# Another order and another choice of engine for the steps of a causal attention with a squared-ReLU layer

## The chip, the cores and the metric

The kernel runs on one core of one Trainium2 chip. The metric is device time in microseconds (us) of one execution; lower is better. Before the change the median of 3 runs is 615.8 us (615.54 to 616.38).

A core has five engines with an instruction queue each: TensorE (PE; its weight loads are shown apart as PEld), VectorE (DVE), ScalarE (ACT), GpSimd (POOL) and SyncE (SP), which issues the transfers. Each works through its own queue in order and waits for the others by semaphores.

## The reference

Causal attention over 4 batches of 12 heads (448 rows, 64 columns per head), then a two-layer block with squared ReLU on the joined heads (1792 rows of 768, 2048 in the middle). All arrays are float32.

```python
scores = scale * np.matmul(q, k.transpose(0, 1, 3, 2))
scores = np.where(mask, -1000000000.0, scores)          # causal
scores = scores - np.max(scores, axis=-1, keepdims=True)
attn = np.exp(scores)
attn = attn / (np.sum(attn, axis=-1, keepdims=True) + 1e-09)
attn_out = np.matmul(attn, v)
x = attn_out.transpose(0, 2, 1, 3).reshape(B * S, H * D)
h = x @ w_in
r = np.maximum(h, 0.0)
return (r * r) @ w_out
```

## The kernel before

**Numbers in halves.** Most operands of a matrix product are float32 values kept as two float16 tiles: a high half, which is the value scaled and rounded, and a low half, which is what the rounding left. A product is three float16 matmuls (high by high, high by low, low by high). Such pairs of steps are made everywhere: of the scaled q and k (tile qs), of v (vp), of the softmax rows (psrc, from the float32 rows pq), of the hidden layer (g, from r), of the weights (wi, wo) and of sums that the last block needs. The function `hi` makes a high half, on ScalarE (line 438) or with one TENSOR_SCALAR on VectorE or GpSimd (line 440). The function `lo` makes a low half. With a fixed scale it is one TENSOR_TENSOR on VectorE or GpSimd (line 446). With a scale per row it is one SCALAR_TENSOR_TENSOR on VectorE (line 451), but two instructions on GpSimd (lines 454 and 456):

```python
            if e == "dve":
                nc.vector.scalar_tensor_tensor(
                    out=out(), in0=in_(), scalar=scale(), in1=top(), op0=ALU.mult, op1=ALU.subtract)
            else:
                nc.gpsimd.tensor_scalar(
                    out=in_(), in0=in_(), scalar1=scale(), scalar2=1.0, op0=ALU.mult, op1=ALU.mult)
                nc.gpsimd.tensor_tensor(out=out(), in0=in_(), in1=top(), op=ALU.subtract)
```

A low half reads its high half, so it comes after it, on whatever engine that was.

**Stages.** The first batch's attention (function `early`, lines 884 to 978) runs while the weights arrive and are narrowed (lines 1022 to 1028), measured and split into halves (lines 1037 to 1115). The two layers of a block of 256 or 128 rows follow (first layer line 1300, second layer line 1319), with the attention of the next batch interleaved: scores (lines 774 and 789), row minimum on VectorE (line 757) with an accumulator read of its own, exponential on ScalarE (line 761), the sum and its inverse on VectorE (lines 801 and 804), the halves of the softmax rows, a transposing transfer (line 676), and the product with v (line 823), read out on VectorE (lines 836 and 839). The last 512 rows are computed with seven products in place of eight (lines 1583, 1685 and 1779), for which VectorE makes sums of weights and rows (line 1455) from the middle of the run on. The scaling of a row of probabilities in `early` is `scaled` (lines 646 and 648), the squares of the hidden layer are lines 1264 and 1266, the copies out of PSUM lines 1257, 1259, 1604 and others.

**What sets the order.** The code first records all 3191 steps with what each reads and writes. It then emits them in the order that a table of numbers, `ORDER`, gives; a second table, `WHERE`, gives the engine of each of the steps that may run on more than one (a ScalarE, d VectorE, g GpSimd). Buffers, transfers, shapes and dependences come from the recording and not from the tables. GpSimd reads and writes SBUF alone; steps with an operand in PSUM go to VectorE or ScalarE.

Of the kernel before, what the change touches and what calls it, by code (L numbers as in the profile page):

```python
# [23 lines left out]
    181 0 2 3 1 4 6 5 11 12 10 176 8 182 183 184 26 27 28 33 31 32 7 9 36 29 34 37 30 35 13 14 15 16 17 18 19 20 186  # L24
    21 22 38 39 40 237 196 50 51 23 24 25 177 53 45 52 201 43 41 56 57 191 44 54 46 47 48 49 42 247 55 178 389 63 58
    64 75 76 388 396 179 65 187 59 82 70 78 68 66 77 81 188 67 79 69 71 238 73 60 80 88 83 72 74 239 189 61 89 62 100
    386 390 84 197 90 387 391 101 240 95 102 103 107 85 91 93 198 98 397 92 94 104 192 105 96 106 99 193 113 180 185
    232 97 202 108 190 114 125 194 109 115 126 248 120 127 132 86 118 128 116 199 119 123 121 252 87 129 195 130 242
    122 138 200 203 124 110 249 139 117 204 145 111 150 140 770 257 151 146 205 152 153 147 157 141 143 112 156 131
    206 148 144 398 399 400 401 402 250 149 207 403 133 404 142 303 158 208 134 405 233 293 159 163 209 154 234 135  # L30
    155 210 164 235 166 406 136 211 253 288 165 407 170 137 213 411 167 214 169 160 243 254 168 244 171 161 258 412
    771 215 162 245 172 413 259 298 395 216 217 304 173 414 416 415 218 294 255 417 260 174 418 175 289 392 313 219
    220 423 393 308 421 290 221 772 773 419 295 424 299 291 222 223 236 241 246 251 224 774 296 305 422 420 342 394
    256 225 226 261 425 435 262 337 436 300 263 437 227 428 438 264 429 306 439 301 228 292 297 440 775 302 307 347
    352 314 229 776 441 265 426 443 444 230 266 777 442 427 779 445 231 446 778 430 315 447 431 787 432 448 309 267
    433 269 270 310 316 343 434 452 271 453 464 362 311 408 268 454 272 348 465 344 357 449 409 455 273 466 457 467
    472 468 312 345 456 349 469 458 353 473 317 274 350 470 275 459 590 363 318 471 354 276 474 462 475 460 463 355
    358 461 319 277 476 364 721 788 278 600 279 493 359 477 494 338 360 481 501 496 280 339 482 365 495 483 281 585
    320 340 497 282 486 595 341 346 351 356 361 366 502 591 484 498 410 592 283 487 485 601 367 450 499 284 488 451
    500 285 503 368 593 489 723 286 504 611 491 212 369 321 370 322 490 371 505 287 492 478 586 602 323 522 789 506  # L40
    587 722 793 724 510 479 725 523 588 325 790 531 480 606 780 511 525 524 507 326 727 530 512 596 603 526 726 513
    327 794 729 515 621 328 597 612 516 514 527 589 528 607 517 627 598 529 508 791 329 728 532 730 731 518 520 792
    799 733 533 616 330 795 521 519 324 608 509 534 535 594 599 331 551 609 539 604 732 734 332 628 540 610 541 735
    613 372 373 333 737 653 800 544 542 545 334 543 552 614 335 736 546 739 801 802 803 336 658 536 622 549 374 547
    835 375 623 617 554 553 796 548 738 806 555 741 624 550 740 376 537 560 797 559 556 568 618 668 743 569 805 812
    576 654 377 571 378 804 784 619 742 557 745 615 655 558 663 577 620 625 379 561 811 605 798 380 562 626 629 538
    669 381 570 807 656 744 630 563 746 836 382 747 817 631 659 749 674 947 813 564 670 632 383 781 814 660 633 572
    815 634 818 384 573 635 748 661 816 637 574 751 750 565 753 695 385 575 679 808 638 566 809 567 671 664 578 824
    579 639 580 752 640 810 581 754 657 582 755 757 665 689 823 675 583 819 820 584 676 680 681 837 666 756 758 759
    821 761 684 825 826 822 641 830 829 682 827 642 760 951 1607 958 950 954 956 955 762 828 838 643 763 662 839 764  # L50
    840 765 644 667 672 881 841 636 645 1609 953 949 882 952 842 843 844 831 1608 832 766 690 782 646 859 850 857 860
    833 647 957 768 691 685 692 677 767 971 696 969 858 686 851 834 965 967 960 964 861 1006 852 678 970 963 959 1003
    1610 862 974 673 972 687 973 876 683 648 769 688 1611 693 1004 649 875 694 697 1007 698 699 966 962 700 849 1001
    1043 863 948 1002 976 1045 650 702 1005 883 874 981 983 864 651 1613 979 873 785 701 977 703 984 652 1033 1034
    1037 1038 961 1044 982 853 978 1077 980 865 1046 705 1008 985 986 989 1047 884 866 1078 1013 1612 877 891 706 987
    994 1036 1011 707 1009 992 1039 1040 1035 867 892 1015 1075 1615 1010 708 968 1076 1012 1014 1016 885 1079 995
    1050 988 993 893 868 894 1017 1107 975 1042 996 783 990 1057 1114 1115 1018 1112 709 1053 1055 896 897 854 1021
    855 1054 710 1051 1052 1058 1026 1056 1616 991 1019 856 711 1146 1113 869 1024 712 898 1020 713 1059 1082 1116
    1041 1619 1060 1147 1025 1027 714 997 1144 870 1110 886 878 1066 1109 1028 1087 1083 1022 1089 1068 998 1090 899
# [1880 lines left out]
```

## Time and profile before

| | us |
|---|---|
| Median of 3 runs | 615.8 |
| Profiled execution, whole | 619.99 |
| its span, first to last instruction | 618.3 |
| TensorE busy | 588.2 (95%) |
| VectorE busy | 565.4 (91%) |
| ScalarE busy | 392.9 (64%) |
| GpSimd busy | 137.4 (22%) |

The profile is of one execution. Its span is 1.7 us shorter than the whole of that execution, and that execution is 4.2 us above the median of the runs. Times within the span count from its first instruction. Ends of matmuls are modelled, so that TensorE can stand as busy while it waits for a short time. TensorE's granted clock is 0.86 of full speed over the first 50 us and 1.00 after that.

### The profile page before, as it was taken

The numbers are of one execution on the slowest core, as the hardware profiler recorded it, in microseconds if no ns is written. First come the engines' busy times: TensorE is split into PE (matmuls) and PEld (weight loads), VectorE is DVE, ScalarE is ACT, GpSimd is POOL, SyncE is SP. The second block draws the span as 40 slices with busy tenths as digits, with TensorE's granted clock in tenths as the row PEclk, the third lists the DMA queues.
The fourth block names the chain that finished last, engine by engine and source line by source line (L and its number), as shares of the span: only waits on it lengthen the run. The fifth ranks groups of instructions, "written<-read, shape, count | busy, mean of one in ns | idle before, by whom it ended". The sixth has DMA issues, their size and how long they took to land. (4 is left out here: it accounts for less than half of the span.)

```text
span 618.3 us, 14173 instructions
## 1 busy us (share of the span) xinstructions
PE 588.2 (95%) x5215; PEld 438.1 (71%) x5215; DVE 565.4 (91%) x1527; ACT 392.9 (64%) x1004; POOL 137.4 (22%) x169
## 2 busy tenths in 40 slices
PE   4789999999999999999989999999999999999997
PEld 2556677888755688767878667777786768886664
DVE  4799999999999898999999998888999999999995
ACT  3688888857884676867878777776535236345420
POOL 1112111312425151231523124162310011100010
PEclk9699999999999999999999999999999999999999
DMA  9879577686668897988988979785340000000003
GB/s 221 263 243 283 191 265 267 211 255 116 139 150 168 190 172 143 210 176 198 208 161 184 177 171 191 156 165 132 65 91 14 27 2 1 14 1 1 1 1 116
DMA packets 207557, 88.71 MB, mean 143 GB/s; under 512 B 192128, under 2 KB 202368, under 8 KB 207488
## 3 DMA queue, kind: packets, MB, share of 16 engines
q1 hardware_dynamic: 207344, 87.71, 59.0%
q8 instruction: 41, 0.67, 0.5%
q14 instruction: 28, 0.23, 0.1%
q10 hardware_dynamic: 144, 0.10, 0.0%
HBM read 49.94 MB, written 5.51 MB: 90 GB/s over the span
## 5 line engine op out<-in xcount | busy, mean ns | idle before, releaser
L1300 PE MATMUL bank<-xt,wi 128*128 128x256 f16 (+1 forms) x1728 | 168.0, 255 | 1.0 <-DVE xt L1222 0.7
L1300 PEld LDWEIGHTS <-wi 128*128 128x128 f16 x1728 | 145.0, 98 | 17.7 <-issue 2.0
L1319 PE MATMUL bank<-wo,g 128*128 128x384 f16 x864 | 151.2, 326 | 0.9 <-ACT xt L1372 0.6
L1319 PEld LDWEIGHTS <-g 128*128 128x128 f16 x864 | 82.2, 98 | 52.2 <-issue 2.3
L761 ACT ACTIVATE pq<-bank,nm 112x336 f32<-112x336 f32 (+3 forms) x144 | 70.1, 491 | 48.8 <-DVE nm L757 41.1
L451 DVE SCALAR_TENSOR_TENSOR psrc<-pq,nm,psrc 112x112 f16<-112x112 f32 (+3 forms) x121 | 62.9, 545 | 1.2 <-ACT psrc L438 0.5
L757 DVE CUSTOM_DVE_ANT_0 bank<-bank,mask,sc 112x112 f32<-112x112 f32 (+3 forms) x96 | 46.9, 510 | 9.2 <-PE bank L774 8.1
L438 ACT ACTIVATE psrc<-pq,nm 112x224 f16<-112x224 f32 (+3 forms) x74 | 36.9, 525 | 8.6 <-DMA pt<-psrc 2.5
L446 POOL TENSOR_TENSOR g<-r,g 128x512 f16<-128x512 f32 x17 | 27.6, 1629 | 47.6 <-ACT g L438 44.9
L774 PE MATMUL bank<-qk 128*112 128x112 f16 (+3 forms) x192 | 32.4, 284 | 2.9 <-ACT pq L761 2.8
L823 PE MATMUL bank<-pt,vp 112*64 112x224 f16 (+3 forms) x504 | 31.1, 268 | 1.1 <-DVE xt L839 0.7
L440 POOL TENSOR_SCALAR psrc<-pq,nm 112x112 f16<-112x112 f32 (+3 forms) x25 | 16.6, 667 | 69.1 <-DVE nm L804 40.4
L823 PEld LDWEIGHTS <-vp 112*64 112x64 f16 x504 | 23.7, 109 | 10.4 <-issue 6.1
L1583 PEld LDWEIGHTS <-wi 128*128 128x128 f16 x288 | 28.2, 98 | 3.9
L761 ACT ACTIVATION_READ_ACCUMULATOR pq<-bank,nm 112x1 f32 x144 | 28.7, 199 | 0.0
L774 PEld LDWEIGHTS <-qk 128*112 128x112 f16 x192 | 21.1, 130 | 10.2 <-issue 5.3
L1264 ACT ACTIVATE r<-r 128x512 f32<-128x512 f32 x37 | 22.9, 626 | 6.0 <-DVE p L466 3.0
L913 DVE CUSTOM_DVE_ANT_0 bank<-bank,mask 128x128 f32<-128x128 f32 (+3 forms) x48 | 21.7, 485 | 5.3 <-PE bank L905 4.8
L1257 ACT ACTIVATE r<-bank 128x512 f32<-128x512 f32 x34 | 20.0, 590 | 7.6 <-DVE g L446 2.5
L757 DVE CUSTOM_DVE_ANT_0 bank<-bank,mask,vst 112x224 f32<-112x224 f32 (+3 forms) x48 | 23.0, 506 | 0.9 <-PE bank L789 0.9
L454 POOL TENSOR_SCALAR pq<-pq,nm 112x224 f32<-112x224 f32 (+3 forms) x23 | 15.6, 679 | 33.9 <-ACT psrc L438 22.7
L905 PE MATMUL bank<-wo 64*96 64x256 f32 (+4 forms) x144 | 18.5, 379 | 3.6 <-ACT wo L654 3.5
(291 smaller groups left out, 1273.7 us busy)
## 6 DMA issues: line engine op xcount, KB each, us to landing
raw<-in_moe_w_out_dram SPq DMA_DIRECT2D x8, 768.0 KB, 4.8
xt<-in_moe_w_out_dram SPq DMA_DIRECT2D x8, 768.0 KB, 5.4
xt<-in_moe_w_in_dram SPq DMA_DIRECT2D x11, 512.0 KB, 5.0
raw<-in_moe_w_in_dram SPq DMA_DIRECT2D x9, 512.0 KB, 4.9
vn<-in_v_dram SPq DMA_DIRECT2D x21, 192.0 KB, 3.0
raw<-in_v_dram SPq DMA_DIRECT2D x18, 224.0 KB, 3.5
out_dram<-ob SPq DMA_DIRECT2D x18, 192.0 KB, 2.2
raw<-in_k_dram SPq DMA_DIRECT2D x12, 224.0 KB, 4.1
```

What stands on the lines that cost most here:

```text
L438: nc.scalar.activation(out=o, in_=i, func=ACTF.Copy, scale=s)
L446: return plan.add({"dve": dve_ns(n), "pool": pool2_ns(n)}, lambda e: engines[e].tensor_tensor(out=out(), in0=in_(), in1=top(), op=ALU.subt ...
L451: nc.vector.scalar_tensor_tensor(out=out(), in0=in_(), scalar=scale(), in1=top(), op0=ALU.mult, op1=ALU.subtract)
L757: one("dve", dve_ns(w, 1, 2) - 52, lambda e: nc.vector.tensor_tensor_reduce(out=s.ap[0:P, 0:w], in0=s.ap[0:P, 0:w], in1=mask[0:P, MZ + P - ...
L761: one("act", act_ns(w, True, 1, True), lambda e: nc.scalar.activation(out=p32[j].ap[0:P, b0 * P:b0 * P + w], in_=s.ap[0:P, 0:w], func=ACTF ...
L774: nc.tensor.matmul(out=s.ap[0:P, 0:(c + 1) * P], lhsT=qT.ap[:, j * NCH + c, :], rhs=kT.ap[:, a:a + c + 1, :].rearrange("p a t -> p (a t)") ...
L823: nc.tensor.matmul(out=pv.ap[j * D:(j + 1) * D, ca * P:t1], lhsT=vp.ap[:, hv, vb:vb + D], rhs=pT[j].ap[0:P, hp * ns + x:hp * ns + x + w, : ...
L913: one("dve", dve_ns(w, 1, 1) - 52, lambda e, c=c, j=j, w=w, ss=ss, nm=nm: nc.vector.tensor_tensor_reduce(out=ss[j].ap[0:M, 0:w], in0=ss[j] ...
L1264: nc.scalar.activation(out=r.ap[:, 0:n], in_=r.ap[:, 0:n], func=ACTF.Square)
L1300: nc.tensor.matmul(out=h.ap[:, y * n:(y + 1) * n], lhsT=wi_hl(ci, hw)[:, mc], rhs=x[:, kd, hx, off:off + n], start=(kd == 0 and hw == 0 an ...
L1319: nc.tensor.matmul(out=o.ap[:, 0:HALF], lhsT=gsl(kf, hg, tt * 128, (tt + 1) * 128), rhs=wo_hl(kf, hw)[:, hh * HALF:(hh + 1) * HALF], start ...
L1583: nc.tensor.matmul(out=ps.ap[:, y * n:(y + 1) * n], lhsT=A[0](f, kd, hw)[:, mc], rhs=B[0](kd, hx), start=(first and y == 0 and kd == 0 and ...
```

## The change

The two tables are replaced; nothing else is touched. The same 3191 steps with the same shapes and dependences stand in another order, and some run on another engine. The diff, cut to the first line of each table:

```diff
 ORDER = """
-    181 0 2 3 1 4 6 5 11 12 10 176 8 182 183 184 26 27 28 33 31 32 7 9 36 29 34 37 30 35 13 14 15 16 17 18 19 20 186
...
 WHERE = (
-    "aagadggaaaagaaaaaaaaagaaaaagagaaaaggaaaaaaaaagaaaaaaaaaaaaaaagaagaaaaaaaaaadgdadadadadgdadadadadadaaagaagaaaaa"
...
+    "aadaaggdaaagagaaaaagaagaaaaaaagaaaggaaaaaaaaggaaaaaaaaaaaaaaaagaaaaaaaaaaaadgdadadadadadadadadadaaaaaaggaaaa"
...
```

328 steps change engine: from VectorE 73 go to ScalarE and 71 to GpSimd, from ScalarE 59 go to VectorE and 50 to GpSimd, from GpSimd 46 go to VectorE and 29 to ScalarE. Each engine's count of instructions at the lines with the largest differences, before and after:

| Engine, line | before | after |
|---|---|---|
| VectorE, 451 (low half) | 215 | 198 |
| VectorE, 440 (high half) | 86 | 69 |
| VectorE, 446 (low half) | 93 | 93 |
| VectorE, 1259 (out of PSUM) | 6 | 3 |
| VectorE, 1604 (out of PSUM) | 4 | 2 |
| GpSimd, 454 and 456 (low half), each | 29 | 46 |
| GpSimd, 440 (high half) | 48 | 70 |
| GpSimd, 648 (scaled row) | 13 | 18 |
| GpSimd, 446 (low half) | 27 | 27 |
| GpSimd, 1266 (square) | 0 | 2 |
| ScalarE, 438 (high half) | 242 | 237 |
| ScalarE, 646 (scaled row) | 38 | 33 |

The order moves on every engine. Two places are shown.

The first is VectorE's queue at the start of the program (wi is the first weight tile, ones_f, ones_b and mask are constants; GpSimd makes the identity matrix ident after mask, and TensorE's first instruction reads ident). Before:

```order
L1858 MEMSET ones_f 128x128
L1860 MEMSET ones_b 128x128
L1861 MEMSET mask 128x240
L1022 TENSOR_SCALAR wi<-g 128x512
L1025 SCALAR_TENSOR_TENSOR wi<-g,wi 128x512
L1028 SCALAR_TENSOR_TENSOR wi<-g,wi 128x512
```

After:

```order
L1022 TENSOR_SCALAR wi<-g 128x512
L1025 SCALAR_TENSOR_TENSOR wi<-g,wi 128x512
L1028 SCALAR_TENSOR_TENSOR wi<-g,wi 128x512
L1858 MEMSET ones_f 128x128
L1860 MEMSET ones_b 128x128
L1861 MEMSET mask 128x240
```

The three instructions that narrow the first weight tile, which wait for its transfer, now stand ahead of the constants.

The second is GpSimd's queue in the middle of the program, where batch 2's rows go through softmax beside the first layers of a block (g and r are the hidden layer, vp and raw belong to v, psrc and pq to softmax). Before:

```order
L440 TENSOR_SCALAR vp<-raw,vst 112x512
L440 TENSOR_SCALAR g<-r 128x2x256
L440 TENSOR_SCALAR qs<-raw,sc 112x8x64
L446 TENSOR_TENSOR g<-r,g 128x2x256 x2
L454 TENSOR_SCALAR pq<-pq,nm 112x112
L456 TENSOR_TENSOR psrc_142<-pq,psrc_142 112x112
```

After:

```order
L440 TENSOR_SCALAR g<-r 128x2x256
L446 TENSOR_TENSOR g<-r,g 128x2x256
L454 TENSOR_SCALAR raw<-raw,vst 112x512
L456 TENSOR_TENSOR vp<-raw,vp 112x512
L440 TENSOR_SCALAR psrc_142<-pq,nm 112x3x112
L446 TENSOR_TENSOR g<-r,g 128x2x256
L440 TENSOR_SCALAR psrc_142<-pq,nm 112x2x112
L440 TENSOR_SCALAR psrc_142<-pq,nm 112x3x112
```

One of the two low halves of g that stood back to back is on VectorE now (it comes after the scores), and a low half of v and high halves of psrc are in the row. VectorE's queue around the same scores (bank is a PSUM bank with scores). Before:

```order
L451 SCALAR_TENSOR_TENSOR psrc_143<-pq,nm,psrc_143 112x3x112
L638 SCALAR_TENSOR_TENSOR sc<-sc 112x1
L440 TENSOR_SCALAR psrc_143<-pq,nm 112x4x112
L451 SCALAR_TENSOR_TENSOR psrc_143<-pq,nm,psrc_143 112x4x112
L757 ISA bank_104,nm<-bank_104,mask,sc 112x112
L757 ISA nm 112x1
L757 ISA bank_112,nm<-bank_112,mask,sc 112x336
```

After:

```order
L451 SCALAR_TENSOR_TENSOR psrc_143<-pq,nm,psrc_143 112x4x112
L451 SCALAR_TENSOR_TENSOR psrc_143<-pq,nm,psrc_143 112x3x112
L451 SCALAR_TENSOR_TENSOR qs<-raw,sc,qs 112x8x64
L638 SCALAR_TENSOR_TENSOR sc<-sc 112x1
L451 SCALAR_TENSOR_TENSOR qs<-raw,sc,qs 112x8x64
L757 ISA bank_104,nm<-bank_104,mask,sc 112x112
L757 ISA nm 112x1
L757 ISA bank_112,nm<-bank_112,mask,sc 112x336
```

The high half of psrc (line 440) stands ten rows further ahead, and two low halves of qs now stand before the row minimum (line 757).

## Rows read from the trace of the kernel before

**Rows 1.** Stretches: PE, PEld, DVE, ACT, POOL busy (count), clock, DMA share, GB/s.

```profile
0.00:50.00 50.00, 35.84 (x241) 23.86 (x242) 36.03 (x128) 33.36 (x101) 6.63 (x19) 0.86 0.85 242
50.00:155.00 105.00, 100.19 (x1068) 81.20 (x1067) 101.49 (x244) 83.27 (x188) 21.82 (x11) 1.00 0.73 227
155.00:450.00 295.00, 287.84 (x2617) 214.67 (x2615) 271.49 (x832) 210.74 (x590) 95.20 (x124) 1.00 0.80 167
450.00:538.00 88.00, 87.71 (x776) 67.43 (x774) 86.80 (x172) 36.64 (x68) 7.85 (x9) 1.00 0.09 21
538.00:618.00 80.00, 76.58 (x524) 50.97 (x521) 69.62 (x156) 28.90 (x59) 5.87 (x8) 1.00 0.07 23
```

**Rows 2.** The chain that ended last: start, us, what. Its last part.

```profile
595.06 19.61 PE bank L1779 x120
614.69 0.62 DVE psrc L1798
```

**Rows 3.** Waits, 155 to 450 us: total us, times, longest.

```profile
PE bank L774 <- ACT pq L761: 2.8, 4, 1.1
DVE qs L451 <- POOL qs L440: 1.1, 2, 0.7
```

**Rows 4.** Whole span, busy (count): lines 451 and 440 (VectorE, GpSimd), 454, 456.

```profile
0.00:618.00 618.00, 130.75 (x215) 0.99 0.60 144
0.00:618.00 618.00, 41.65 (x86) 36.13 (x48) 0.99 0.60 144
0.00:618.00 618.00, 21.02 (x29) 0.99 0.60 144
0.00:618.00 618.00, 23.84 (x29) 0.99 0.60 144
```

**Rows 5.** A group by shape, VectorE: count, busy us, mean ns, idle before.

```profile
L451 DVE SCALAR_TENSOR_TENSOR psrc<-pq,nm,psrc 112x112 f16<-112x112 f32 x29 | 11.3, 394 | 0.1
```

**Rows 6.** Timeline, GpSimd beside VectorE: start, us, instruction, idle before and releaser.

```profile
263.86 2.59 POOL L446 TENSOR_TENSOR g<-r,g 128x512 f16<-128x512 f32 x2 [1.21 <-DVE sc L472]
264.23 1.11 DVE L638 SCALAR_TENSOR_TENSOR sc<-sc 112x1 f32<-112x1 f32 x1
265.27 1.42 DVE L440 TENSOR_SCALAR psrc<-pq,nm 112x448 f16<-112x448 f32 x1
268.25 0.54 PE L774 MATMUL bank<-qk 128*112 128x448 f16 x2 [0.85 <-ACT pq L761]
...
306.93 0.15 DVE L638 SCALAR_TENSOR_TENSOR sc<-sc 112x1 f32<-112x1 f32 x1
...
401.56 0.45 DVE L440 TENSOR_SCALAR psrc<-pq,nm 112x448 f16<-112x448 f32 x1
```

**Rows 7.** Timeline: the first and the last lengthened VectorE instruction of 155 to 450 us.

```profile
160.79 0.34 DVE L440 TENSOR_SCALAR psrc<-pq,nm 112x112 f16<-112x112 f32 x1
448.98 1.98 DVE L1455 TENSOR_TENSOR pq<-wi 128x512 f32<-128x512 f16 x2
```

**Rows 8.** Timeline: the same, first and last, of 450 to 538 us.

```profile
495.53 1.16 DVE L446 TENSOR_TENSOR raw<-pq,raw 128x512 f16<-128x512 f32 x1
532.73 1.25 DVE L440 TENSOR_SCALAR xt<-pq 128x512 f16<-128x512 f32 x1
```

**Rows 9.** Timeline of the start.

```profile
0.88 0.17 DVE L1858 MEMSET ones_f<- 128x128 f32 x1 [0.88 <-PEq L1924]
1.18 0.26 DVE L1861 MEMSET mask<- 128x240 uint32 x1
2.03 0.29 POOL L1866 TENSOR_SCALAR_AFFINE_SELECT ident<-ident 128x128 f32<-128x128 f32 x1
6.17 0.74 DVE L1028 SCALAR_TENSOR_TENSOR wi<-g,wi 128x512 uint16<-128x512 uint32 x1
6.47 1.09 PE L884 MATMUL bank<-ident,wo 128*128 128x128 f32 x4 [6.47 <-DMA wo<-in_q_dram]
19.21 0.43 DVE L1022 TENSOR_SCALAR wi<-g 128x512 int32<-128x512 int32 x1 [1.41 <-DMA g<-in_moe_w_in_dram]
```

More of the change, by code (lines that the diff above doesn't have):

```diff
@@ L23 @@
 ORDER = """
[131 rows of a table removed]
[131 rows of a table added]
 """
 WHERE = (
-    "aagadggaaaagaaaaaaaaagaaaaagagaaaaggaaaaaaaaagaaaaaaaaaaaaaaagaagaaaaaaaaaadgdadadadadgdadadadadadaaagaagaaaaa"
-    "aaaaaaaaaaaaaaaaaaaaaaaaaaaaaaaaaaaaaaaaaaaaaaaaadadadadadadadadadadadadddddadadadaaagaaagaaadaaadaaadaaadaaag"
-    "aaagaaadaaagaaddaaagaaadadadadgdddgdaadadadgdagadadaadddgdgdddadadagdgdadadgdaddgagdadddggaddgaddadadadgdadada"
-    "daadddddadddddadaagddadgdadadaddagadgdadgdagdgaadaggdddadddddaadadadddaddddddddadgdadddadddaaadddaagdaagaagdaa"
-    "agdaadaaggaadgaaadaddaaaadaaagaaadaaadaaaddaadaaggdaddaaaaaaaaddddaddgddadddgdadagadaadgddgadddadadadadadagdad"
-    "ddddddgdaddddddgggadaadgdddadadadgdaggdadddaadgdadddgdadadggaggdadaadddadadddddadddadddaddaaggaaagdddgaaadaaag"
-    "aaagaadgadaddaaaaaaaadadaaadaaadaaadaddaddadddgdadadddddadadadaagadagddgggdddddagadaddadadadadagadddagadggddda"
-    "dadgdadddddadggdgadagdddadadgdadddddadddgdagdadadddddadgdddadadadddaagddadadadadddadadddadadadddadadddagadadad"
-    "ddadagadgdadadadgdadddaaaadaaaadaaaddaagadaaaaadaaddgddddaaadaaadagdaaddddaaadaaddaaaadaaadagdaaaaddadgdadadad"
-    "adadadagadadadadadadadadadagddadadagadaddgddaddgadadaadaadaaaadd"
+    "aadaaggdaaagagaaaaagaagaaaaaaagaaaggaaaaaaaaggaaaaaaaaaaaaaaaagaaaaaaaaaaaadgdadadadadadadadadadadaaaaaaggaaaa"
+    "gaaaagaaaaaaaaagaaaaaaaaaaaaaagaaagaaaaaaaaaaaaaaaadadadadadadadadgdadadadadadadadagagaaagaaagaaadaaadaaadaaag"
+    "aaadaaagaadgaaagaaadaaadadddgdgdddadaadadadgddgadadaadgdaggdadgdadaadadadgdgdaggdaadgdadddadggddaadaggdadagada"
+    "gdddadadagadaddgaadgdggadddgdaddadadadagadgdaddggadgdagadaddddadagadadadadddaggaddggdadadddaaaadaadgaagdaadgaa"
+    "addaadaddgaaadaaaaadaaaaadaaagaaggaaagaagddaddaaagaaadaaaadadaddddgdaggdgdaddgadadagdadadadgdadgdadgdgddgadaag"
+    "ddggddadadadgdadgdadaadadadddagddadgggdggadaadgdadddadagaggdadgddgdadadadggadgdddadddaddddaadgaaagaaddaadddaad"
+    "aaddagagaaaddaaaaaaaadgdaaddaaadaaadaaadgdddddggadadddgdggadadaddddaggdgggdgdagddagadaddadadadadddddgdddgdagda"
+    "dadadgdadggdddgadadggdddgdaddgggaddgaggdagadaadgdaddggdgdddagadddadaddddadadgdadddddadadadadadadddadadgdagadad"
+    "adadgdadadadadagagadadaaaadaaaagaddadaagadadaaagaaadaadaaagadaaadagdaaaagdaaadaddaadaadaaadaadaaadgdagaddgadag"
+    "adadadadadddddadagddadddadadadagddadadddddddddadadadaaddaaadadaa"
 )
```

261 rows, old and new, of the table ORDER are left out of this document.

## The prediction

> **What bounds the kernel now.** I read the stretches first, since the shares of the whole run (TensorE 95%, VectorE 91%) mix stages with different limits. TensorE stands idle for 50.00 - 35.84 = 14.2 us in the first 50 us, 4.8 us from 50 to 155, 7.2 us from 155 to 450, 0.3 us from 450 to 538 and 3.4 us from there on [rows 1]. That is all that an order can give back, short waits inside "busy" time apart, because the matmuls themselves are the same. The chain says what the last stretch is: 19.6 us of matmuls with nothing between, then one VectorE step at 614.69 and its store [rows 2]. The 3.4 us there lie behind the last matmul, and no step before it can shorten them. So the end is fixed, and 450 to 538 has 0.3 us to give: a gain must come from the time before 450.
>
> From 50 to 155 VectorE is busy for 101.5 of 105 us and TensorE waits for its weights and rows: VectorE is the bound. From 155 to 450 it is busy for 271.5 of 295, so it is idle for 23.5 us, and TensorE for 7.2. Neither is full; the two hold each other up. TensorE's named waits there end most of all on an exponential of ScalarE, line 761 (2.8 us in four waits) [rows 3], which in turn waits for VectorE's row minimum. An in-order VectorE queue that is behind makes these waits.
>
> Why it is behind can be seen once in full. From 263.86 GpSimd makes two low halves of g, 2.59 us. Line 638 on VectorE, one column wide, takes 1.11 us in place of 0.15, and the high half after it 1.42 in place of 0.45. The row minima come 1.9 us late, and at 268.25 TensorE has waited 0.85 us for the exponential [rows 6]. By the Trainium skill's page "SBUF — State Buffer", section "Who interferes with whom", VectorE and GpSimd have a pair of SBUF ports in common, and a VectorE instruction with two SBUF inputs or in a two-port mode keeps the other out or is kept out until the first is done; these rows agree.
>
> I added up this loss over the trace, each VectorE instruction against the median of its shape without GpSimd beside it. Five instructions before 155 us lose 1.6 us beside 28.4 us of GpSimd (0.06 us per us); 48 from 155 to 450 lose 19.1 beside 95.2 (0.20) [rows 1, 7]; five from 450 to 538 lose 2.5 beside 7.9 (0.32) [rows 1, 8]. At 263.86 it is 1.9 beside 2.59 (0.75), the worst place.
>
> **The change, part by part.** The shapes are the same, so rows of before price nearly all of it.
>
> VectorE loses 17 low halves (line 451) and 17 high halves (line 440) net. At the lines' means, 130.75 / 215 = 0.61 and 41.65 / 86 = 0.48 us [rows 4], that is 18.5 us. The means hold the lengthening, and the shapes that leave are rather small (a low half of 112 columns takes 0.39 us [rows 5]). Taking each instruction at the undisturbed spacing of its own shape, the two lines give 14.1 us and the few copies out of PSUM that leave 3.9, together 18.0. By the place of the steps in TensorE's order, 15.9 us of them leave the stretch 155 to 450, 2.6 the stretch to 538; before 155 VectorE has 0.4 us more, at the end 0.5 more.
>
> GpSimd gains 17 low halves of two instructions, 0.72 + 0.82 us, and 22 high halves at 36.13 / 48 = 0.75 [rows 4]: 26 + 17 us. With five scaled rows and two squares it is about 44 us at undisturbed lengths: 30 us from 155 to 450, 10 before 155, 4 after. This lies beside VectorE, so its own length costs nothing while a low half is not waited for; what it costs is VectorE's time at the port. ScalarE changes by under 4 us in any stretch and is idle for 84 of the 295 us: nothing [rows 1].
>
> 155 to 450: VectorE loses 15.9 us and gets back 30 x 0.20 = 6.0, so it has 9.9 us less to do, and its idle time goes from 23.5 to 33.4 us. If TensorE's waits shrink only as that slack grows, they go from 7.2 to 7.2 x 23.5 / 33.4 = 5.1 (-2.1). If the new order takes every one away, -7.2. The place above speaks for more than the first: one of its two low halves goes to VectorE, and the high half goes ahead. I take the middle, **-4.6**.
>
> Added waits: high halves on GpSimd whose low half is on VectorE go from 38 to 54 (counted in the two orders), and behind a VectorE instruction that waits so stand row minima. The 38 cost VectorE 1.1 us in line 451 [rows 3], so 16 more cost about 0.5 us of its 33 idle ones. It is inside the range. A low half on GpSimd also delays its transposing transfer by 0.72 + 0.82 - 0.61 = 0.9 us; SP's queue holds as many transfers as before, so I set no cost.
>
> Before 155: GpSimd's 9.4 us more between 50 and 155 lie beside a VectorE that is the bound. At 0.06 it is **+0.6**, at 0.32 +3.0. I take the first, since it is this stretch's own rate, and keep the other for the range.
>
> The start: the mask constant is done at 1.44 and ident 0.88 us later [rows 9]. Now the constants stand behind the first narrowing, which ends at about 6.9. The 0.56 us from the first constant's start to the last one's end then run to 7.4 and ident at 8.3, so TensorE's first matmul comes at 8.3 in place of 6.47: 1.8 us. VectorE later waits for weight tiles anyway (1.41 us before 19.21), and these waits swallow a delay. Between 0 and 1.8 I take **+0.5**.
>
> After 450: 0.3 us at stake, **0**. Sum: -4.6 + 0.6 + 0.5 = -3.5, so 616.5 for the profiled execution of 619.99. The median stands 4.2 us below that: 615.8 - 3.5 = **612.3 us**.
>
> **The rivals.** *The relief does not reach TensorE.* The waits are chains of score, minimum, exponential, and VectorE's new slack is spent waiting for TensorE and ScalarE. Then -2.1 + 1.1 = -1.0: 614.8. For it: VectorE is idle for 23.5 us even now. Against: row 268.25, where the delay is VectorE's own.
>
> *GpSimd's new work holds VectorE up* (slower). Place: 50 to 155 above all. Price at 0.32: +3.0, with ident's full 1.8; and in the middle 15.9 - 9.6 = 6.3 us less, idle 29.8, TensorE's waits 5.6 (-1.5). Sum +3.3: 619. It decides from the point where the start costs more than the middle gives; in the middle alone nothing is left at 15.9 / 30 = 0.53 us per added GpSimd us, between 0.20 of the stretch and 0.75 of the worst place. The skill's page "Perfetto Trace Analysis", section "Optimizing Scalar/DVE Operations", warns of just this: work moved between these two engines might not help, as they have a port in common. By the trace it costs a fifth of a us per us on average; if, as the rule allows, every added us held VectorE for its whole length, VectorE would have 30 - 15.9 = 14.1 us more in the middle, 9.4 idle, TensorE's waits would be 18 and the time about 627. I give that 0.03, within this rival's chance.
>
> *More comes back.* The 14.2 us of idle TensorE in the first 50 us are waits between engines and for transfers, which an order can shorten, too. If 2 us come back there and all 7.2 in the middle: 615.8 - 9.2 + 1.1 = 607.7. Against it: VectorE's work ahead of each matmul up to 155 us, added up along both orders, differs by under 2 us.
>
> **How the numbers follow.** Forecast (609.5 to 614.5): 0.42. More comes back: 0.16. No relief: 0.20. Held up: 0.22. About 0.2%, 1.2 us, is what a measurement of this kernel can tell from no change. Faster 0.58, within 0.2% 0.20, slower 0.22. The range for 8 in 10 reaches from 606 to 619.
>
> **What would show it.** Right: from 155 to 450 TensorE idle about 3 us, VectorE busy about 10 us less, GpSimd about 30 more, VectorE's loss per GpSimd us at 0.20 or below. Wrong: that rate above 0.5; or TensorE's work of the first 155 us done later than before; or a first matmul later than 8.3 us whose delay is still there at 155. If VectorE is relieved and TensorE's waits stay, the first rival holds.

## The result and the profile after

The changed kernel takes 609.32 us (median of 4 runs, 608.95 to 609.83), the kernel before, beside it, 615.69 us (615.54 to 616.38). The ratio is 0.9895, with an interval of 0.9878 to 0.9912: about 6.5 us, or 1.05%, faster. The forecast was 612.3 us. Its direction holds, and the time lies in the range of 606 to 619, just below the narrower band of 609.5 to 614.5; the gain is nearly twice the 3.5 us that were summed up. The sum hides more than that: a stretch that gained about 10 us, and one that lost about 4.

The profiled execution of the changed kernel takes 609.83 us, its span 608.0. The stretches of the kernel after, with the columns of [rows 1] (start and end, length, busy us and count of PE, PEld, DVE, ACT and POOL, granted clock, DMA share, GB/s):

```profile
0.00:50.00 50.00, 36.09 (x272) 24.84 (x273) 37.67 (x133) 35.02 (x104) 7.07 (x20) 1.00 0.86 254
50.00:155.00 105.00, 99.97 (x1063) 81.56 (x1061) 99.23 (x244) 81.54 (x190) 37.26 (x17) 0.98 0.72 222
155.00:450.00 295.00, 294.41 (x2679) 219.50 (x2677) 261.64 (x809) 213.00 (x585) 121.44 (x178) 1.00 0.80 169
450.00:538.00 88.00, 87.58 (x777) 69.33 (x775) 81.94 (x160) 41.83 (x77) 11.67 (x12) 1.00 0.03 10
538.00:618.00 80.00, 66.36 (x437) 42.46 (x434) 60.15 (x146) 22.13 (x45) 4.94 (x5) 0.98 0.06 23
```

The last row reaches past the end of the span at 608.0, so its clock and its busy shares are not those of work.

From 155 to 450 us TensorE is idle for 295 - 294.41 = 0.6 us, where [rows 1] had 7.2. From 50 to 155 it is idle for 5.0 us, and the granted clock there is 0.98 where it was 1.00.

The waits of 155 to 450 us after (total us, times, longest), against [rows 3]. TensorE's first, it is the only one; then three of VectorE's:

```profile
PE bank L774 <- ACT pq L761: 0.5, 1, 0.5
...
DVE bank L757 <- PE bank L774: 7.8, 16, 1.4
...
DVE psrc L451 <- POOL psrc L440: 2.7, 3, 1.3
DVE qs L451 <- POOL qs L440: 1.9, 1, 1.9
```

VectorE now waits most of all for TensorE's scores: it is early. It also waits 4.6 us for high halves on GpSimd, where [rows 3] had 1.1. No wait of TensorE comes of it.

The last part of the chain after, against [rows 2] (start, us, what), is the same 120 matmuls without a gap, 10.1 us earlier:

```profile
584.92 19.51 PE bank L1779 x120
```

Of these 10.1 us nearly 5 belong to the profiled execution of before and not to the change. A second profile of the unchanged kernel (`before_again`) takes 615.17 us, with a granted clock of 1.00 from the start, where [rows 1] shows 0.86 over the first 50 us. Its first three stretches:

```profile
0.00:50.00 50.00, 37.46 (x267) 25.21 (x268) 38.69 (x136) 35.97 (x107) 6.93 (x19) 1.00 0.89 255
50.00:155.00 105.00, 101.67 (x1118) 83.31 (x1117) 102.50 (x256) 84.99 (x196) 24.76 (x14) 1.00 0.72 226
155.00:450.00 295.00, 287.52 (x2594) 214.25 (x2592) 271.65 (x819) 207.49 (x578) 94.94 (x123) 1.00 0.79 167
```

The middle is that of [rows 1] to 0.4 us. I compare with this second profile from here on, and with medians for times.

**Where the time went.** TensorE has the same matmuls in both kernels, in another order, so one can ask of each trace when the same amount of matmul work was done. How the matmuls of each shape are weighted shifts single figures of this reading by about 1 us. The changed kernel minus the second profile of before: 1.9 us later at the first matmul; 0.5 us earlier at 10 us of work; level at 30 to 60; then 2.1 us later at 80, 5.2 at 104, 4.0 at 140; 1.7 later at 200, 1.5 earlier at 300, 5.6 earlier at 440, and 5.4 earlier at the end. So it loses 4 to 5 us between 60 and 104 us of work (84 to 136 us of time), and gains nearly 10 from there to 440. After that hardly anything moves. The experiments ask why for both.

### The profile page after: what moved, and what is told of

Read it like the earlier page. It is cut to its first block, busy times and chain, and to the rows that moved or that the text cites. A ratio compares the mean times of both kernels' runs of the same rounds, so it can differ in the third digit from the quotient of the medians.

```text
span 608.0 us, 14265 instructions
## 1 busy us (share of the span) xinstructions
PE 584.4 (96%) x5215; PEld 437.7 (72%) x5215; DVE 540.6 (89%) x1488; ACT 393.5 (65%) x997; POOL 182.4 (30%) x232
## 4 chain that ended last, share of the span: by engine, by line
PE 70%; DVE 20%; DMA 3%; POOL 2%; ACT 2%; issue 2%; DVEq 0%; SPq 0%; ACTq 0%; POOLq 0%
PE bank L1319 25%; PE bank L1300 23%; DVE pq L1455 5%; PE bank L823 4%; PE bank L1779 4%; PE bank L774 4%; PE bank L1685 2%; DVE bank L913 2%; DVE wi L1025 2%; DVE wi L1028 2%; POOL psrc L648 2%; PE bank L789 2%; PE bank L1583 2%; PE bank L961 1%; PE bank L945 1%
## 5 line engine op out<-in xcount | busy, mean ns | idle before, releaser
L761 ACT ACTIVATE pq<-bank,nm 112x448 f32<-112x448 f32 (+3 forms) x144 | 70.1, 490 | 37.9 <-DVE nm L757 36.7
L451 DVE SCALAR_TENSOR_TENSOR psrc<-pq,nm,psrc 112x448 f16<-112x448 f32 (+3 forms) x108 | 57.5, 556 | 4.2 <-POOL psrc L440 2.7
L440 POOL TENSOR_SCALAR psrc<-pq,nm 112x112 f16<-112x112 f32 (+3 forms) x43 | 23.3, 552 | 66.9 <-DVE nm L804 47.7
L438 ACT ACTIVATE psrc<-pq,nm 112x448 f16<-112x448 f32 (+3 forms) x70 | 36.1, 541 | 8.0 <-DVE nm L804 3.2
L446 POOL TENSOR_TENSOR g<-r,g 128x512 f16<-128x512 f32 x15 | 20.4, 1360 | 60.2 <-ACT g L438 40.1
L913 DVE CUSTOM_DVE_ANT_0 bank<-bank,mask 128x256 f32<-128x256 f32 (+3 forms) x48 | 21.8, 485 | 6.7 <-PE bank L905 6.5
L648 POOL TENSOR_SCALAR psrc<-psrc,nm 128x256 f32<-128x256 f32 (+3 forms) x9 | 21.7, 2425 | 18.8 <-DVE nm L930 12.3
L454 POOL TENSOR_SCALAR pq<-pq,nm 112x112 f32<-112x112 f32 (+3 forms) x36 | 19.6, 543 | 25.7 <-ACT psrc L438 15.1
L456 POOL TENSOR_TENSOR psrc<-pq,psrc 112x112 f16<-112x112 f32 (+3 forms) x36 | 25.5, 708 | 3.0
L757 DVE CUSTOM_DVE_ANT_0 bank<-bank,mask,vst 112x112 f32<-112x112 f32 (+3 forms) x48 | 22.7, 509 | 0.5 <-PE bank L789 0.5
```

The costliest lines, as they stand in the source:

```text
L438: nc.scalar.activation(out=o, in_=i, func=ACTF.Copy, scale=s)
L451: nc.vector.scalar_tensor_tensor(out=out(), in0=in_(), scalar=scale(), in1=top(), op0=ALU.mult, op1=ALU.subtract)
L648: engines[e].tensor_scalar(out=out(), in0=in_(), scalar1=scale(), scalar2=1.0, op0=ALU.mult, op1=ALU.mult)
L757: one("dve", dve_ns(w, 1, 2) - 52, lambda e: nc.vector.tensor_tensor_reduce(out=s.ap[0:P, 0:w], in0=s.ap[0:P, 0:w], in1=mask[0:P, MZ + P - ...
L761: one("act", act_ns(w, True, 1, True), lambda e: nc.scalar.activation(out=p32[j].ap[0:P, b0 * P:b0 * P + w], in_=s.ap[0:P, 0:w], func=ACTF ...
L913: one("dve", dve_ns(w, 1, 1) - 52, lambda e, c=c, j=j, w=w, ss=ss, nm=nm: nc.vector.tensor_tensor_reduce(out=ss[j].ap[0:M, 0:w], in0=ss[j] ...
```

## The experiments

All are edits of the two tables. Ratios are to the kernel before, measured beside each; a difference of ratios of 0.001 is 0.6 us.

| Kernel | median us | ratio (95% interval) |
|---|---|---|
| changed kernel | 609.32 | 0.9895 (0.9878 to 0.9912) |
| `where_only` | 638.33 | 1.0359 (1.0345 to 1.0373) |
| `order_only` | 643.90 | 1.0459 (1.0438 to 1.0480) |
| `consts_first` | 608.44 | 0.9870 (0.9852 to 0.9887) |
| `row_to_scalare` | 606.11 | 0.9838 (0.9825 to 0.9852) |
| `both_mended` | 604.11 | 0.9817 (0.9803 to 0.9831) |
| `old_start` | 605.18 | 0.9834 (0.9821 to 0.9848) |
| `new_start` | 618.10 | 1.0026 (1.0013 to 1.0039) |
| `three_pieces` | 605.63 | 0.9817 (0.9801 to 0.9834) |
| `relief_undone` | 612.33 | 0.9952 (0.9939 to 0.9965) |
| `weights_behind` | 610.40 | 0.9898 (0.9878 to 0.9918) |

### The unchanged kernel again

> The kernel before, profiled a second time, because its first profiled execution was 4.2 us above the median and its granted clock 0.86 over the first 50 us, where the changed kernel's was 1.00. If the extra belongs to that execution's start, this one has a clock near 1.00 there, a span near 614 us and the same idle TensorE of about 7 us from 155 to 450. If the extra lies in the middle, TensorE's idle time from 155 to 450 is about 3 us here, and most of the profile's difference in the middle was chance.

615.17 us, rows above. Where equal TensorE work is done, the first profile of before is 3.1 us behind the second by 50 us and 5.0 behind by 110 us (there it waits 1.6 us for a transfer); after that the distance stays. So the extra lies in the first 110 us, most of it in the start, and none in the middle.

### One table alone

Both edits are shown against the changed kernel, by the first line of the table. New engines in the old order (`where_only`):

```diff
 ORDER = """
-    181 182 183 184 0 2 3 4 1 6 5 11 12 7 26 176 13 10 9 14 8 27 33 34 35 28 36 29 37 31 32 30 15 16 17 18 19 20 21 22
+    181 0 2 3 1 4 6 5 11 12 10 176 8 182 183 184 26 27 28 33 31 32 7 9 36 29 34 37 30 35 13 14 15 16 17 18 19 20 186
...
```

> The new choice of engines in the old order. Relief theory (VectorE has 18 us less to do, whatever the order): 611 to 614 us, VectorE busy 8 to 12 us less than before. Placement theory (GpSimd's work pays only where the order puts it beside VectorE work that does not need the shared port): VectorE's loss per GpSimd us is 0.20 or more, TensorE waits for late GpSimd halves, 615 to 622 us.

New order with the old engines (`order_only`):

```diff
 WHERE = (
-    "aadaaggdaaagagaaaaagaagaaaaaaagaaaggaaaaaaaaggaaaaaaaaaaaaaaaagaaaaaaaaaaaadgdadadadadadadadadadadaaaaaaggaaaa"
+    "aagadggaaaagaaaaaaaaagaaaaagagaaaaggaaaaaaaaagaaaaaaaaaaaaaaagaagaaaaaaaaaadgdadadadadgdadadadadadaaagaagaaaaa"
...
```

> The new order with the old choice of engines. Relief theory: VectorE has its 18 us of work back, so most of the gain is gone, 614 to 617 us. If the order alone makes the gain, 609 to 611 us. Placement theory: the old GpSimd steps stand where they were not planned, 615 to 622 us.

Both are slower than either kernel, by 22 and 28 us against the kernel before, and slower than any of the theories had them. From 155 to 450 us, first of `where_only`, with its first wait of TensorE (the table is ten lines longer in this file, so line 774 stands as 784 and 761 as 771):

```profile
155.00:450.00 295.00, 277.33 (x2446) 204.34 (x2444) 256.80 (x770) 206.21 (x576) 123.93 (x169) 1.00 0.78 165
...
PE bank L784 <- ACT pq L771: 7.6, 13, 1.4
```

and of `order_only` (nine lines longer):

```profile
155.00:450.00 295.00, 274.53 (x2370) 200.12 (x2370) 253.07 (x779) 198.59 (x556) 86.88 (x117) 0.99 0.75 160
...
PE bank L783 <- ACT pq L770: 8.7, 14, 2.4
```

TensorE is idle there for 17.7 and 20.5 us, and the largest named part of it, 7.6 and 8.7 us, is for the same exponential as in [rows 3]. So neither table is worth anything by itself, and no term of the gain belongs to one of them alone. That an order is good only for the engine times that it was made for is the reading nearest at hand; what makes up the 22 and the 28 us was not taken apart.

`where_only` shows more. It gives GpSimd almost what the changed kernel gives it (123.9 and 121.4 us in the stretch). I added up the loss of VectorE as the prediction did, each instruction against the median of its shape without GpSimd beside it. It is 27.7 us in `where_only` and 12.4 us in the changed kernel: 0.22 and 0.10 us for each us of GpSimd. The row shows in the mean ns of a shape (the number ahead of the bar). A low half of 112x512 and one of 112x336, VectorE, from 155 to 450 us, in `where_only` (line 461 here):

```profile
L461 DVE SCALAR_TENSOR_TENSOR psrc<-pq,nm,psrc 112x336 f16<-112x336 f32 x25 | 17.1, 684 | 0.7 <-ACT psrc L448 0.7
...
L461 DVE SCALAR_TENSOR_TENSOR qs<-raw,vst,qs 112x512 f16<-112x512 f32 x5 | 4.8, 963 | 0.0
```

and in the changed kernel:

```profile
L451 DVE SCALAR_TENSOR_TENSOR psrc<-pq,nm,psrc 112x336 f16<-112x336 f32 x27 | 16.2, 604 | 1.7 <-ACT psrc L438 0.9 <-POOL psrc L440 0.7
...
L451 DVE SCALAR_TENSOR_TENSOR qs<-raw,vst,qs 112x512 f16<-112x512 f32 x5 | 3.7, 749 | 1.1 <-ACT qs L438 0.8 <-issue 0.3
```

The same steps on the same engines lose 684 - 604 = 80 ns and 963 - 749 = 214 ns more each in the old order. What differs is which VectorE instruction runs beside GpSimd. Worked out from the instruction records, 155 to 450 us: us of VectorE beside GpSimd, and in brackets the us that those instructions lost (medians of each shape are taken over all traces of this case, so the sums differ by a few tenths from those above; VectorE instructions that follow each other overlap a little in the trace, so the us beside GpSimd add up to more than GpSimd's busy time):

| VectorE line | before (second profile) | changed | `where_only` |
|---|---|---|---|
| 757, row minimum, reads PSUM | 31.1 (0) | 62.2 (0) | 42.5 (0) |
| 451, low half | 30.3 (5.8) | 33.5 (6.6) | 55.8 (16.7) |
| 440, high half | 12.7 (5.7) | 5.2 (0.6) | 8.8 (3.3) |
| all lines | 104.0 (18.7) | 130.0 (12.4) | 134.4 (27.3) |

All of the additional GpSimd time, and some that was there, lies beside the row minima, which read their scores from PSUM and lose nothing. By the Trainium skill's page "SBUF — State Buffer", section "Who interferes with whom", a VectorE instruction with at most one SBUF input, outside the two-port modes, doesn't contend with GpSimd; the 62.2 us with no loss agree. Over all traces of this case, where a VectorE low half has just one GpSimd instruction beside it, a subtraction there costs it 0.38 us per us, a scaling 0.09 (line 440) or nothing (line 454). That is well short of one engine being kept out for as long as the other works, which the prediction allowed for.

The place of [rows 6] in the changed kernel (start, us, instruction) shows it once:

```profile
263.46 1.16 POOL L446 TENSOR_TENSOR g<-r,g 128x512 f16<-128x512 f32 x1 [6.26 <-DVE g L440]
...
263.68 0.69 DVE L757 CUSTOM_DVE_ANT_0 bank<-bank,mask,sc 112x448 f32<-112x448 f32 x1 [0.30 <-PE bank L774]
...
264.30 0.86 DVE L446 TENSOR_TENSOR g<-r,g 128x512 f16<-128x512 f32 x1
...
265.09 0.14 DVE L638 SCALAR_TENSOR_TENSOR sc<-sc 112x1 f32<-112x1 f32 x1
```

The one low half of g that is left on GpSimd lies beside a row minimum, and both have their undisturbed lengths (1.16 and 0.69 us). Line 638, which took 1.11 us in [rows 6], takes 0.14, and the wait of 0.85 us is gone.

### Start and rest exchanged

`old_start` has order and engines of the kernel before for the first 770 steps (104 us of TensorE's work, 132 us of time), then the changed ones. `new_start` is the reverse. As one edit, n being the 770:

```diff
-order = changed
+order = before[:n] + [i for i in changed if i not in before[:n]]      # old_start
+order = changed[:n] + [i for i in before if i not in changed[:n]]     # new_start
```

> Order and engines of the kernel before for the first 770 steps of the plan (TensorE work of about 104 us, up to about 132 us of time), then order and engines of the changed kernel for the rest. Theory A, the start loses 4.2 us and the middle gains 9.6 us, each by itself: 609.3 - 4.2, so 604.5 to 606, and TensorE's idle time from 155 to 450 us stays near 0.6 us. Theory B, the middle gains because the changed start leaves it a better place (work put off or done ahead): the gain of the middle shrinks by what the start wins, 608 to 612.

> The fourth corner: order and engines of the changed kernel for the first 770 steps, and of the kernel before for the rest. If start and rest add, the time is that of before plus the start's loss of 4.2 to 5.2 us, so 619 to 621, and TensorE's idle time from 155 to 450 us is near 7.5 us again. If the old rest makes up for a late start, it is 615 to 617.

By ratios, in us against before: changed -6.5, `old_start` -10.2, `new_start` +1.6. So the rest gains 10.2 us behind the old start and 8.1 behind the new one, and the new start costs 3.7 ahead of the new rest and 1.6 ahead of the old one. `old_start` came out as the first theory had it. `new_start` was to lie at 619 to 621 and lies at 618.1. Direction and place hold. The two prices of the start are 2.1 us apart, where the intervals of the three ratios allow for about 1.5 by chance; what the rest of it is stays open. From 155 to 450 us, of `old_start` and of `new_start`:

```profile
155.00:450.00 295.00, 294.44 (x2664) 219.31 (x2662) 261.92 (x799) 211.69 (x579) 119.92 (x176) 1.00 0.79 168
```

```profile
155.00:450.00 295.00, 287.12 (x2583) 213.40 (x2578) 271.17 (x821) 207.82 (x580) 95.49 (x124) 1.00 0.80 166
```

TensorE's idle time there is 0.6 us with the new rest and 7.9 with the old one, whichever the start is. The gain of the middle belongs to the middle.

### The constants in second place

```diff
 ORDER = """
-    181 182 183 184 0 2 3 4 1 6 5 11 12 7 26 176 13 10 9 14 8 27 33 34 35 28 36 29 37 31 32 30 15 16 17 18 19 20 21 22
+    181 0 182 183 184 2 3 4 1 6 5 11 12 7 26 176 13 10 9 14 8 27 33 34 35 28 36 29 37 31 32 30 15 16 17 18 19 20 21 22
```

> The changed kernel with the step that sets the constants back in second place, ahead of the narrowing of the first weight tile. TensorE's first matmul then comes at about 6.5 us in place of 8.28. If later waits swallow the delay (the traces' progress of TensorE is equal again after 10 us of its work), the time stays at 609.3 within 0.5 us; if the delay is carried through, 607.5 us.

In the changed kernel the start is as forecast: mask at 7.09, first matmul at 8.28.

```profile
7.09 0.26 DVE L1861 MEMSET mask<- 128x240 uint32 x1
```

```profile
8.28 1.12 PE L884 MATMUL bank<-ident,wo 128*128 128x128 f32 x4 [8.28 <-POOL ident L1866]
```

With the constants in second place it comes at 6.96, not at 6.5, since it then waits for its transfer. Taking these 1.3 us of delay away brings 0.0025 of the ratio, 1.5 us: by the medians the delay is carried through. The intervals overlap, but the same edit on top of the next one (`both_mended` against `row_to_scalare`) brings 0.0021, 1.3 us, and in the traces `consts_first` is about 1.3 us ahead of the changed kernel from 50 to 100 us of TensorE work. At the end of these two executions it is 0.5 us ahead.

### One scaled row back on ScalarE

The stretch that loses has one odd row. GpSimd, VectorE and TensorE around it, timeline of the changed kernel:

```profile
97.18 11.18 POOL L648 TENSOR_SCALAR psrc<-psrc,nm 96x352 f32<-96x352 f32 x2 [4.74 <-DVE nm L930]
```

```profile
108.42 0.55 PE L945 MATMUL bank<-ident,psrc 96*128 96x96 f32 x4 [2.55 <-POOL psrc L648]
```

```profile
113.14 0.29 DVE L1115 TENSOR_REDUCE wst<-bank 128x1 f32<-128x128 f32 x1 [4.01 <-PE bank L1109]
```

Of the two scaled rows the first takes 0.9 us and the second 10.3 (98.06 to 108.36); both ran on ScalarE before, in under 0.6 us each. TensorE waits 2.55 us for it, then VectorE 4.01 us for TensorE. Two stretches of the same trace:

```profile
105.90:108.40 2.50, 0.00 (x0) 0.00 (x0) 2.50 (x6) 0.65 (x2) 2.50 (x2) 1.00 0.83 335
...
109.00:112.50 3.50, 3.50 (x27) 2.82 (x28) 0.13 (x3) 1.65 (x4) 1.60 (x2) 0.51 0.00 0
```

Behind the 2.5 us in which TensorE did nothing, its granted clock is 0.51, the lower of its two levels (1.2 of 2.4 GHz), for 3.5 us, in which it is busy all the time. The second of the two rows goes back to ScalarE:

```diff
 WHERE = (
...
-    "gaaaagaaaaaaaaagaaaaaaaaaaaaaagaaagaaaaaaaaaaaaaaaadadadadadadadadgdadadadadadadadagagaaagaaagaaadaaadaaadaaag"
+    "gaaaagaaaaaaaaagaaaaaaaaaaaaaagaaaaaaaaaaaaaaaaaaaadadadadadadadadgdadadadadadadadagagaaagaaagaaadaaadaaadaaag"
```

> The changed kernel with one entry of its table of engines taken back: one early scaled row of 96x352 (line 648, psrc) runs on ScalarE, as before the change, and not on GpSimd; the order is the changed one. In the trace of the changed kernel this step takes 10.3 us on GpSimd (98.06 to 108.36) beside weight steps of VectorE that stand one behind the other, TensorE waits 2.55 us for it at 108.42, its clock then falls to half for 3.4 us, and VectorE waits 4.01 us for TensorE at 113.14. Theory A, this one late step is what the stretch 50 to 155 us loses (4.2 us against the kernel before, read where equal TensorE work is done): the time falls by 3.5 to 4.5 us, to 605 or 606, and the half clock and both waits are gone. Theory B, the stretch loses by the order of its TensorE work, and the late step only fills time that is lost anyway: 608.5 to 610, and another wait stands at the same place.

One letter of the table brings 0.0057 of the ratio, 3.5 us: 606.11. From 50 to 155 us of that kernel the clock is 1.00 again, and TensorE is busy for 2.2 us more, all of it at full clock:

```profile
50.00:155.00 105.00, 102.20 (x1123) 83.45 (x1122) 102.84 (x257) 84.29 (x196) 29.03 (x18) 1.00 0.73 228
```

With the constants in second place as well (`both_mended`, the two diffs above together):

> The changed kernel with the constants' step taken back to the second place of the order and the scaled row at 98 us taken back to ScalarE, and nothing else. If the two losses add: 608.4 (the run with the constants' step alone) less 3.5 to 4.5, so 604 to 605, 1.7 to 1.9% under the kernel before. If the late row costs nothing by itself: 608 to 609.

604.11 us: the two losses add. With `three_pieces` below, which has the same ratio, this is the fastest version, 1.8% under the kernel before and 0.8% under the changed one.

`new_start` has the same late step, and TensorE the same wait:

```profile
96.61 11.17 POOL L648 TENSOR_SCALAR psrc<-psrc,nm 96x352 f32<-96x352 f32 x2 [4.74 <-DVE nm L930]
```

```profile
107.83 0.55 PE L945 MATMUL bank<-ident,psrc 96*128 96x96 f32 x4 [2.55 <-POOL psrc L648]
```

```profile
110.96 0.29 DVE L1115 TENSOR_REDUCE wst<-bank 128x1 f32<-128x128 f32 x1 [2.42 <-PE bank L1109]
```

But in this trace the clock stays at 1.00, and VectorE waits 2.42 us in place of 4.01. `consts_first` and `relief_undone` keep the step on GpSimd, too; there it takes 10.3 us, TensorE waits 2.6 and 2.5 us, and half clock follows in both. So in the changed order the late step and the wait come every time, the half clock in three traces of four; why not in the fourth stays open. The two prices of the start are hardly explained by it: one such stretch of half clock takes 0.003 from an execution's mean clock, and 8 of the 12 executions of `new_start` have a mean of 0.997 or less, as have 3 of the 4 of the changed kernel. The clock fell somewhere in most of them as well.

### What held the row up

While GpSimd worked for 10.3 us at one row, VectorE did almost nothing but weight steps, back to back: narrowing (lines 1022, 1025, 1028) and low halves (451). If they starve it (keep it waiting over and over while it is under way), the row must be short where they are not. `weights_behind` leaves the row on GpSimd and moves the narrowing of four tiles behind the two exponential steps of line 913 (the numbers are steps of the plan: 547 and 549 are line 913, the eight of the second added line that narrow are 609, 614, 622, 617, 623, 618, 624, 619):

```diff
 ORDER = """
...
-    545 609 543 801 795 734 736 555 737 546 739 334 509 653 614 335 806 372 336 622 556 796 617 738 623 741 797 374
-    610 557 615 558 628 802 560 658 812 740 375 618 624 376 561 803 743 536 619 377 562 537 563 742 745 378 547 663
-    668 620 625 549 373 605 695 805 548 804 798 626 550 538 629 654 568 379 630 744 811 747 569 655 380 564 807 659
+    545 543 801 795 734 736 555 737 546 739 334 509 335 806 372 336 556 796 738 741 797 374 557 558 628 802 560 812
+    740 375 376 561 803 743 536 377 562 537 563 742 745 378 547 549 609 653 614 622 617 623 610 615 658 618 624 619
+    663 668 620 625 373 605 695 805 548 804 798 626 550 538 629 654 568 379 630 744 811 747 569 655 380 564 807 659
```

> The changed kernel with every engine as changed, the scaled row of 96x352 at 98 us still on GpSimd, and one thing moved in the order: the eight steps of VectorE that narrow four output weight tiles (lines 1022, 1025 and 1028, 98.5 to 107.2 us) stand behind the two exponential steps of line 913 at 107.83 and 108.37, with what hangs on them. Theory A, these weight steps starve the GpSimd step: it takes under 3 us instead of 10.3, nobody waits for it, and unless the late weights cost something of their own the time is 605 to 608. Theory B, the step is slow by itself at this place, whatever VectorE does: it takes 8 us or more again.

GpSimd's queue in that kernel (timeline), and TensorE's first wait from 90 to 160 us:

```profile
95.17 1.43 POOL L648 TENSOR_SCALAR psrc<-psrc,nm 96x352 f32<-96x352 f32 x2 [4.74 <-DVE nm L930]
104.30 8.61 POOL L446 TENSOR_TENSOR g<-r,g 128x512 f16<-128x512 f32 x2 [7.71 <-ACT g L438]
```

```profile
PE bank L1109 <- DVE wo L1025: 4.0, 1, 4.0
```

Both rows together take 1.43 us where they took 11.18; the second alone takes 0.55 in place of 10.3. The starving went with the weight steps: the next two low halves, now beside them, take 8.61 us, where the changed kernel needs 2.3 for them. The first theory holds for the row. The time didn't fall, 610.4 us, because TensorE now waits 4.0 us for the late weights; that price I had left open. Nor is it new: the kernel before and `old_start` have such a step, too, for which nobody waits. Here `old_start`, where 1.16 us is the undisturbed length:

```profile
107.08 4.84 POOL L446 TENSOR_TENSOR g<-r,g 128x512 f16<-128x512 f32 x1 [5.06 <-ACT g L438]
```

### The relief taken back

`relief_undone` puts the 52 halves that went from VectorE to GpSimd between 170 and 420 us back, in the changed order (in the engine table 52 times):

```diff
-g
+d
```

> The changed kernel in its changed order, with the 52 steps (38 low halves, 14 high halves, 170 to 420 us) that the change moved from VectorE to GpSimd in the middle put back on VectorE; every other entry stays as changed. In the trace of the kernel before these steps take 28.9 us on VectorE, in that of the changed kernel 67.9 us on GpSimd. Theory A, the middle gains because VectorE is relieved: VectorE's busy time from 155 to 450 us rises by about 29 us, less the loss by GpSimd that falls away (0.10 us for each us of GpSimd, some 7 us), to some 284, which leaves next to no slack in a stretch of 295 us; TensorE's idle time there returns and passes that of before (7.5 us), and the time is 616 to 625. Theory B, the gain of the middle is the order's, and the engine of these steps hardly counts: 607 to 611, with TensorE's idle time there under 2 us.

612.33 us, 3.5 us slower than the changed kernel by ratios: between the two theories (616 to 625, 607 to 611). For the same TensorE work (140 to 440 us of it), first the second profile of before, then the changed kernel, then `relief_undone`:

```profile
169.20:485.70 316.50, 309.10 (x2791) 230.93 (x2789) 292.60 (x855) 209.88 (x569) 89.17 (x115) 1.00 0.71 151
```

```profile
173.20:480.00 306.80, 306.21 (x2771) 228.46 (x2770) 273.21 (x812) 209.36 (x559) 114.55 (x167) 1.00 0.73 157
```

```profile
172.60:484.90 312.30, 307.89 (x2772) 229.16 (x2771) 289.90 (x868) 210.59 (x560) 53.26 (x83) 1.00 0.72 154
```

The 52 steps give VectorE 289.9 - 273.2 = 16.7 us more, not 22, and TensorE needs 5.5 us more for the work in this execution. VectorE is then as busy as before the change (289.9 and 292.6), yet the work is done 316.5 - 312.3 = 4.2 us sooner. So the relief carries a part of the middle's gain: 3.5 us by the medians of the 8 to 10 that the rest gives, 5.5 of 9.7 in these profiled executions, of which that of `relief_undone` is 1.9 us above its median. The other part, more than half by the medians, comes with the order and the other exchanges of steps between the engines; which of them, this run doesn't tell, and `order_only` shows that they can't be had one by one.

### A version of three pieces

Changed start to step 528 with the constants in second place, then the order of before to step 770, then the changed one:

```diff
-order = changed
+a = changed_constants_second[:528]
+b = [i for i in before[:770] if i not in a]
+order = a + b + [i for i in changed if i not in a + b]
```

> A version put together from the stretches that each kernel does better: changed order and engines for the first 528 steps with the constants in second place, then order and engines of before up to step 770 (so the two scaled rows at 97 and 98 us are on ScalarE), then the changed ones for the rest. Read where equal TensorE work is done, the mended start is 2.0 to 2.8 us ahead of before at 72 to 76 us of TensorE work, the old piece keeps that to 104 us, and the rest gains about 10 us: 602 to 603.5. If stretches don't add so finely, 604 to 606, as the versions before it.

605.63 us, and the ratio 0.9817 is that of `both_mended`. The 602 to 603.5 read off the stretches didn't come. At 80 us of TensorE work `both_mended` is 2.2 us ahead of the second profile of before, this version 0.2 us behind. Part of that is its profiled execution's clock, 0.86 over the first 25 us:

```profile
0.00:25.00 25.00, 15.29 (x86) 10.04 (x88) 13.36 (x57) 12.43 (x40) 3.13 (x14) 0.86 0.92 258
```

But the median has no gain either. By this one trace the lead is lost near the first seam; no other run shows it. Gains of a start and a rest could be added to within 2 us; those of a stretch of 20 us could not.

## Why the prediction was right, and where not

**Place: right.** The gain lies before 450 us and in the middle, the end is fixed, and the two exchanged halves show that middle and start are apart. That the time fell into the range is in part luck: the middle gave 3.5 to 5.6 us more than its term, the start and the stretch behind it cost 0.5 to 2.6 more than their 1.1, and the two errors offset each other.

**155 to 450 us, -4.6: right in kind, too small.** Measured, the rest gives -8.1 to -10.2. The step that failed first is the price of GpSimd's time. I took the stretch's own mean, 0.20 us for each added us, and had VectorE lose 6.0 us more. It lost 6.7 less (19.1 to 12.4), since the price isn't one of GpSimd's time but of its partner: nothing beside line 757, 0.38 beside a low half. [Rows 6] showed one partner, and I used it for the size of the worst place only; the list of lengthened instructions behind [rows 7] had the partners' lines, and I added it up to one number. By the prediction's own rule the right price would still have given only -5.4: VectorE's idle time 23.5 + 15.9 + 6.7 = 46.1 us, TensorE's waits 7.2 x 23.5 / 46.1 = 3.7 (-3.5), and the middle between that and -7.2. The larger part is the next point. "VectorE busy about 10 us less" came out to a tenth (271.5 to 261.6) and for the wrong reason: the stretch after holds more of the work. At equal work VectorE has 292.6 - 273.2 = 19.4 us less.

**How far TensorE's waits shrink: undersized.** I took the middle between "as the slack grows" and "every one". Nearly every one went (7.5 to 0.6 from 155 to 450 us). And the bound of 7.2 was none: at equal work 6.8 us of idle time and 309.1 - 306.2 = 2.9 us of "busy" went. The prediction named short waits inside "busy" apart and then left them out. Over the whole span TensorE's busy time goes from 586.1 us (second profile) to 584.4, though 3.5 us of the latter are at half clock; the mean lengths of the large groups by line are the same, so they don't show where those waits lay.

**50 to 155 us, +0.6: wrong by its mechanism.** The stretch costs 1.6 to 3.7 us, start included. I looked for VectorE lengthened by GpSimd, and there is hardly any (1.3 us beside 37.3). It went the other way round: VectorE starved GpSimd, and the GpSimd step had a TensorE matmul behind it. One such step is worth 3.5 us (`row_to_scalare`). "Its own length costs nothing while a low half is not waited for" was right as a sentence; who waits for the five scaled rows that moved wasn't looked up. It is the place of the rival "GpSimd's new work holds VectorE up" without its mechanism.

**The start, +0.5:** first matmul at 8.28 as worked out (8.3). 1.3 us of the delay were taken away, and 1.3 to 1.5 us came back, so by the medians later waits swallow little of it: between 0 and 1.8 it is nearer to the upper end than I took it. **After 450, 0:** right, 0.2 us.

**The rivals.** "More comes back" (607.7) came nearest in time, and its middle (-7.2) was nearer than the forecast's; its 2 us in the first 50 did not come (TensorE idle for 13.9 us there, 12.5 in the second profile of before). "Relief does not reach TensorE" is refuted by the middle.

## What to carry to other kernels

Price work that moves to GpSimd by the VectorE instruction that it will lie beside, not by the stretch's mean: beside instructions that read PSUM it was free here, beside two-input steps on SBUF a subtraction cost 0.38 us per us. And look at the price from the other side: a GpSimd step beside a row of VectorE weight steps took 10.3 us for 0.6, so nothing that TensorE waits for goes there. After a change of so many steps, read the trace of its result for single steps far above their shape's length; one letter of the table was worth half of what the whole change brought.

## What was unexpected of the hardware

- One GpSimd TENSOR_SCALAR of 96x352 was held for 10.3 us through more than a dozen VectorE instructions that followed each other (0.55 us is its shortest length in these traces, in `weights_behind`). A fit over the GpSimd instructions of this case's traces gives the time that GpSimd loses for each us beside a VectorE line: 1.0 to 1.2 beside lines 1028 and 1025, about 0.5 beside 451, under 0.1 beside 757 and 913.
- After 2.5 us without a matmul the granted clock was at half for 3.5 us in the changed kernel's trace, and so it was in `consts_first` and `relief_undone` (2.6 and 2.5 us); in that of `new_start` it stayed at 1.00 after the same pause. In `weights_behind` it went to half after a wait of 4.0 us. Of two profiles of the kernel before, one had half clock in its first 50 us (mean 0.86) and the other none, with 619.99 and 615.17 us.
